# Last block of attention: scores issued two and a half key tiles ahead of the sums of values instead of one and a half

## The chip, the cores and the metric

One NeuronCore of a Trainium2 chip runs the whole program. The metric is the time of one execution on the device in microseconds (us); lower is better. TensorE (PE in the profile) does the matrix products, with its weight loads shown apart (PEld); VectorE is DVE, ScalarE is ACT, GpSimd is POOL, and SyncE (SP) issues most of the DMAs.

## The reference

Two layers in a row, each an attention block followed by an MLP block, with the same weights both times. x is 2048 rows of 640 numbers, there are 32 heads of 20 numbers each, and the MLP is 1536 wide.

```
def _A_ref(x, wqkv, wo):                      # attention
    qkv = (x @ wqkv).reshape(B, S, 3, H, Dh).transpose(2, 0, 3, 1, 4)
    q, k, v = qkv[0], qkv[1], qkv[2]
    scores = einsum("bhqd,bhkd->bhqk", q, k) * (Dh ** -0.5)
    p = softmax(scores, axis=-1)
    o = einsum("bhqk,bhkd->bhqd", p, v)
    return o.transpose(0, 2, 1, 3).reshape(B, S, D) @ wo

def _B_ref(x, w1, b1, w2, b2):                # MLP
    h = relu(x @ w1 + b1)
    return (h * h) @ w2 + b2

for _ in range(2):
    x = x + _A_ref(layernorm(x), A_wqkv, A_wo)
    x = x + _B_ref(layernorm(x), B_w1, B_b1, B_w2, B_b2)
```

## The kernel before, in words

**Stages.** Each layer runs `qkv` (projections), `attention`, then the output projection (`add_heads`) and the MLP (`mlp`). Most operands are kept as a high and a low part, and products are summed from three partial products.

**Blocks of attention.** The work is cut into 32 blocks: 8 groups of four heads times 4 blocks of 512 queries. A block goes over 16 key tiles of 128 keys. For one key tile of a block, TensorE makes the scores of the four heads (each a matrix of 128 keys by 512 queries, one PSUM bank each), ScalarE takes their exponential into a buffer `e` in SBUF, and TensorE then multiplies that with the values and adds to the block's accumulator in PSUM bank 7 (`pv`, line 567: four instructions, one for each head, which the profile counts as eight). A column of ones beside the values gives the sum for the softmax's division. The maxima of the scores, which are subtracted ahead of the exponential, come from a second set of products (line 473) that VectorE reduces; they are made ahead of the block that uses them.

**Order.** The program is written out by hand; each engine runs its instructions in the order written and waits at semaphores. Blocks 0 to 30 follow the strings in `ORDERS`, in which a and b are score products (line 555), m and n are products for the maxima, and V is the sum of values of one key tile. There a score bank is read by one exponential of 512 columns (line 562).

**The last block (31).** When it begins, all maxima are made, so their banks 4 to 6 are free. The block uses `both_heads(p)`: two score products side by side (line 1065) into a pair of banks, and one exponential of 1024 columns over that pair (line 1072). This is called a half here, since it is half of a key tile (two of the four heads); halves are numbered 0 to 31, and half 2k + p belongs to key tile k. Three pairs of banks are used in turn (line 1061), so half n writes the pair that the exponential of half n − 3 has read. Six buffers `e` are used in turn (line 1059), so the exponential of half n writes the buffer that the sum of key tile (n − 6)/2, rounded down, has read.

```
state["bank"] = (state["bank"] + 2) % 6
dst = banks[:, state["bank"] : state["bank"] + 2, :]
```

Halves 0 and 1 are issued among the last instructions of block 30 (line 1098). Line 1102 then issues half 2, and the loop of lines 1103 to 1107 issues the sum of one key tile and then two halves, until the halves run out.

**What hangs on the last block.** `both_heads` calls `begin(i)` when it comes to a new key tile; that writes out the DMAs and the small steps that are due there: the rest of block 30's division (`finish`: a load, a power of −1 on GpSimd, a spread, a gather, a multiplication and a store, at the tiles 4, 6, 7, 9, 11 and 12 after block 30's end), loads of finished heads (`heads`), and at tile 12 four rows of x for the output projection. SyncE takes the DMAs in that order and waits only for what each of them needs. After the block, `add_heads` multiplies the heads with `wo` (line 285 for TensorE, line 1138 for VectorE's addition to x).

Of the kernel before, what the change touches and what calls it, by code (L numbers as in the profile page):

```python
# [39 lines left out]
def tile_layers(  # L40
# [899 lines left out]
    def attention(first, x_src, first_rows):  # L940
# [27 lines left out]
        def begin(i):  # L968

            t, u = divmod(i, NKT)  # L970
            g, qb = divmod(t, NQB)
            if u == 1:
                q_t.pop(t - 1, None)
                if t + 2 < NBLK and t + 2 not in q_t:
                    load_q(t + 2)
            if u % 4 == 1 and qb == 0:
                k_t.pop((g - 1, u // 4), None)
                for h in (0, 1, 2, 3) if g else (0, 1, 2):
                    if g + h < NG and (g + h, u // 4) not in k_t:
                        load_k(g + h, u // 4, True)  # L980
                if g and g + 3 >= NG:
                    del kept[(g - 1) % 4, u // 4]
            if t == 1 and u % 4 == 1:
                load_k(3, u // 4, True)
            if u in (2, 10) and qb == NQB - 1 and g + 1 < NG:
                load_v(g + 1, u // 8)
            if first and t < 16 and u % 6 == 3:
                prep_job()
            if first and t < 16 and u == 8:
                for sp in (w_o, w_1, w_2):  # L990
                    sp.save_full()
                    sp.past(sp.count, sp.got)
            if (t, u) in loads:
                loads[t, u]()
            if t == NBLK - 1 and u == 12:
                first_rows.extend(row_tile(x_src, i) for i in range(4))
            if i in split:
                split.pop(i)()
# [52 lines left out]
        def both_heads(p):  # L1051

            i = state["wide"]
            t, kt = divmod(i, NKT)
            if p == 0 and i > state["begun"]:
                state["begun"] = i
                begin(i)
            es = es_of.setdefault(i, {})
            es[p] = weights[len(e_n) % len(weights)]
            e_n.append(t)  # L1060
            state["bank"] = (state["bank"] + 2) % 6
            dst = banks[:, state["bank"] : state["bank"] + 2, :]
            for par in range(2):
                b = 64 * par
                nc.tensor.matmul(  # L1065
                    dst[:, par, :],
                    k_t[t // NQB, kt // 4][b : b + 62, p, (kt % 4) * P : (kt % 4 + 1) * P],
                    q_t[t][b : b + 62, p, :],
                    start=True,
                    stop=True,  # L1070
                )
            nc.scalar.activation(es[p], dst, AF.Exp, scale=SCALE)  # L1072
            if p:
                state["wide"] += 1
# [24 lines left out]
                else:  # L1099
                    op(o)  # L1100
        assert min(sm_n) == len(todo) and spare == 4
        both_heads(0)
        while state["done"] < last:
            op("V")
            for p in (1, 0):
# [128 lines left out]
    def layer(first, x_a, x_m, x_e, front_0, ahead):  # L1234
        qkv(first, x_a, front_0)
        xs = []
        attention(first, x_a, xs)
        steps = []
        for i in sorted(split):
# [161 lines left out]
```

## Time and profile before

| | |
|---|---|
| median of 3 runs | 3659.83 us (3656.69 to 3662.13) |
| the profiled execution's own time | 3659.64 us |
| its span in the profile | 3657.8 us |
| clock granted to TensorE, mean | 0.998 |
| last block, layer 1 | 1382.40 to 1425.86 us of the span |
| last block, layer 2 | 3197.62 to 3241.06 us of the span |

The two stretches of the last block are counted from the start of the first exponential of 1024 columns to the end of the last sum of values. The profile gives the busy time of each engine, groups of instructions with their mean time, the chain of work that ended last, and rows in order of time. A row of the timeline gives the start, the length, the engine, the line, the operation with output and inputs, the shapes, how many instructions it joins, and in brackets how long the engine was idle just before and what ended that. A merged row ends where its last instruction ends.

### The profile page before, as it was taken

Reading aid. Unit: us, or ns where it says so; the run is one execution under the profiler, and the core shown is the slowest. Engines: PE = TensorE matmul, PEld = TensorE weight load, DVE = VectorE, ACT = ScalarE, POOL = GpSimd, SP = SyncE. Lnnn points to the kernel's source line nnn. Section 1 sums busy time; section 2 is a strip of 40 time slices with the busy share of each in tenths; the row PEclk is TensorE's granted clock in tenths of the full one; section 3 lists DMA queues with packets and bytes.
Section 4 is the critical chain, followed back from the end, with each engine's and each line's share of the span. In section 5 each row is a group of like instructions: output and inputs, shape, how many; then the busy total and the mean of one; then the engine's idle time right before and its main releaser. Section 6 shows DMA issues by size and latency. Waiting matters only on the chain.

```text
span 3657.8 us, 67630 instructions
## 1 busy us (share of the span) xinstructions
PE 3604.9 (99%) x25770; PEld 2153.4 (59%) x25770; DVE 2725.1 (75%) x5039; ACT 2645.2 (72%) x5131; POOL 819.4 (22%) x909
## 2 busy tenths in 40 slices
PE   8999999999999998999999999999999999989999
PEld 7886333343333435999888963334444343369998
DVE  7878999999999992344567789999999999723443
ACT  2778999999999994122227789999999999931221
POOL 6531434211221121111164201211211221101110
PEclk9999999999999999999999999999999999999999
DMA  8866545323211135511277652232232111364111
GB/s 268 279 228 175 170 145 159 102 68 79 56 46 47 50 102 191 208 44 44 80 254 253 205 149 69 70 79 59 64 79 58 44 47 42 110 239 151 44 48 39
DMA packets 254451, 425.03 MB, mean 116 GB/s; under 512 B 60354, under 2 KB 107202, under 8 KB 254126
## 3 DMA queue, kind: packets, MB, share of 16 engines
q1 hardware_dynamic: 253310, 418.35, 36.9%
q8 instruction: 202, 3.31, 0.4%
q10 hardware_dynamic: 816, 2.36, 0.2%
q14 instruction: 123, 1.01, 0.1%
HBM read 260.73 MB, written 159.88 MB: 115 GB/s over the span
## 4 chain that ended last, share of the span: by engine, by line
PE 95%; DVE 2%; ACT 2%; POOL 1%; issue 0%; DMA 0%; SPq 0%; ACTq 0%; DVEq 0%; POOLq 0%
PE banks L567 28%; PE banks L555 19%; PE banks L473 16%; PE banks L285 12%; PE banks L321 10%; PE banks L1201 9%; ACT e L1072 1%; PE banks L1160 0%; DVE mx L485 0%; PE banks L392 0%; PE banks L1065 0%; ACT e L562 0%; DVE bst L243 0%; DVE h L256 0%; DMA q<-d_qk 0%
## 5 line engine op out<-in xcount | busy, mean ns | idle before, releaser
L562 ACT ACTIVATE e<-banks 128x512 f32<-128x512 f32 x3968 | 2049.5, 604 | 65.7 <-PE banks L473 6.8
L485 DVE TENSOR_REDUCE mx<-banks 128x1 f32<-128x512 f32 x3076 | 1931.4, 684 | 212.6 <-PE banks L473 140.7
L473 PE MATMUL banks<-k,q 60*128 60x512 f32 x3587 | 1244.6, 428 | 3.2 <-DVE mx L485 1.4
L567 PE MATMUL banks<-e,vg 128*32 128x512 f32 x8192 | 1091.8, 605 | 29.7 <-ACT e L1072 28.8
L555 PE MATMUL banks<-q,k 62*128 62x512 f32 x3968 | 1118.1, 434 | 1.0 <-DVE mx L502 0.3
L555 PEld LDWEIGHTS banks<-q,k 62*128 62x128 f32 x3968 | 583.8, 185 | 657.3 <-ACT e L562 625.3
L473 PEld LDWEIGHTS banks<-k,q 60*128 60x128 f32 x3587 | 582.0, 184 | 291.6 <-DVE mx L485 217.1
L502 DVE CUSTOM_DVE_ANT_0 rl<-banks,rl 128x512 f32<-128x512 f32 x511 | 333.6, 689 | 102.3 <-PE banks L473 93.5
L567 PEld LDWEIGHTS banks<-e,vg 128*32 128x32 f32 x8192 | 161.2, 108 | 389.9 <-issue 324.8
L321 PE MATMUL banks<-xnT,wqk 64*128 64x512 f32 x2400 | 382.8, 396 | 3.4 <-DVE xnT L256 1.2
L1201 PE MATMUL banks<-w,h 128*128 128x320 f32 x2304 | 349.4, 310 | 0.8 <-DVE h L256 0.7
L494 ACT ACTIVATE rl<-banks 128x512 f32<-128x512 f32 x515 | 273.6, 598 | 101.5 <-PE banks L473 93.3
L1201 PEld LDWEIGHTS banks<-w,h 128*128 128x128 f32 x2304 | 339.3, 188 | 2.5 <-DVE h L256 1.3
L285 PE MATMUL banks<-xnT,w 128*128 128x512 f32 x1440 | 330.0, 389 | 0.0
L1186 ACT ACTIVATE r<-banks,b_t 128x512 f32<-128x512 f32 x96 | 66.2, 689 | 352.8 <-PE banks L285 351.4
L321 PEld LDWEIGHTS banks<-xnT,wqk 64*128 64x128 f32 x2400 | 289.3, 187 | 37.9 <-issue 2.3
L285 PEld LDWEIGHTS banks<-xnT,w 128*128 128x128 f32 x1440 | 269.6, 188 | 55.1
L267 POOL CAST mr<-nt 128x32 fp32r<-128x32 f32 x64 | 13.4, 209 | 1121.5 <-DVE nt L528 1121.3
L611 POOL TENSOR_TENSOR few<-few,minus_t 128x16 f32<-128x16 f32 x62 | 179.8, 2900 | 234.8 <-DMA few<-d_s 234.8
L321 PE MATMUL banks<-wv,xnT 64*128 64x320 f32 x1920 | 199.7, 307 | 0.9 <-ACT mark_t L323 0.9
L321 PEld LDWEIGHTS banks<-wv,xnT 64*128 64x128 f32 x1920 | 187.9, 185 | 2.6 <-ACT mark_t L323 1.6
L1212 DVE TENSOR_TENSOR x<-banks,x 128x320 f32<-128x320 f32 x128 | 62.1, 492 | 168.3 <-PE banks L1201 165.4
(80 smaller groups left out, 2050.9 us busy)
## 6 DMA issues: line engine op xcount, KB each, us to landing
q<-d_qk SPq DMA_DIRECT2D x242, 240.0 KB
d_qk<-ev SPq DMA_DIRECT2D x80, 512.0 KB
k<-d_qk SPq DMA_DIRECT2D x152, 240.0 KB
x<-d_x SPq DMA_DIRECT2D x88, 320.0 KB
d_qk<-ev SPq DMA_DIRECT2D x80, 256.0 KB
d_o<-ot SPq DMA_DIRECT2D x248, 80.0 KB
ot<-d_o SPq DMA_DIRECT2D x38, 512.0 KB
d_v<-v SPq DMA_DIRECT2D x32, 512.0 KB
```

Source lines behind the costliest of these rows:

```text
L285: nc.tensor.matmul(dst, a, b, start=(n == 0), stop=(n == last))
L321: m = nc.tensor.matmul(ch["dst"][:, :width], *pair, start=first, stop=last)
L473: nc.tensor.matmul(dst, q_t[t][b : b + 60, p, sub * P : (sub + 1) * P], k_t[t // NQB, c][b : b + 60, p, :], start=True, stop=True,)
L485: nc.vector.tensor_reduce(maxima(t)[:, 2 * par + p, sub, c : c + 1], dst, axis=AX.X, op=ALU.max)
L494: nc.scalar.activation(res, dst, AF.Relu)
L502: nc.vector.tensor_tensor_reduce(out=r, in0=dst, in1=r, scale=1.0, scalar=LEAST, op0=ALU.add, op1=ALU.max, accum_out=maxima(t)[:, 2 * par ...
L555: nc.tensor.matmul(dst, k_t[t // NQB, kt // 4][b : b + 62, p, (kt % 4) * P : (kt % 4 + 1) * P], q_t[t][b : b + 62, p, :], start=True, stop ...
L562: nc.scalar.activation(es[p][:, par, :], dst, AF.Exp, scale=SCALE)
L567: nc.tensor.matmul(acc[32 * h : 32 * h + 32, :], v_t[t // NQB, kt // 8][:, kt % 8, 32 * h : 32 * h + 32], es[p][:, par, :], start=(kt == 0 ...
L611: nc.gpsimd.tensor_tensor(few, few, minus_t, op=ALU.pow)
L1186: nc.scalar.activation(r, dst, AF.Relu, bias=b1_t[:, f : f + 1])
L1201: nc.tensor.matmul(dst[:, :HALF], hs[f][:, hx, i * P : (i + 1) * P], w_2.piece(at_2(f0 + f, hw, hf)), start=(f == 0 and (hx, hw) == THREE[0]),
```

## The change

One call of `both_heads` ahead of the loop becomes three: half 2, half 3 and half 4 are issued before the sum of key tile 0, where it was half 2 alone. The loop itself is the same, so from there on every sum of key tile k stands behind the halves up to 2k + 4, where it stood behind those up to 2k + 2. The banks, the buffers and the number of instructions are the same. `begin` is called one key tile earlier in relation to the sums; nothing moves in the order of ScalarE, VectorE, GpSimd or SyncE.

```
         assert min(sm_n) == len(todo) and spare == 4
-        both_heads(0)
+        for p in (0, 1, 0):
+            both_heads(p)
         while state["done"] < last:
             op("V")
             for p in (1, 0):
                 if state["wide"] < last:
                     both_heads(p)
```

TensorE at the start of layer 1's last block, before (L567 is the sum of values, four instructions for a key tile; L1065 the scores, two instructions for a half; the first two rows are the last sum of block 30):

```order
L567 MATMUL banks<-e_4750,vg_14074 32x512 x2
L567 MATMUL banks<-e_4749,vg_14074 32x512 x2
L1065 MATMUL banks<-q_14198,k_5125 128x512 x2
L567 MATMUL banks<-e_4752,vg_13921 32x512 [waits DVE_49,Activation_49]
L567 MATMUL banks<-e_4752,vg_13921 32x512
L567 MATMUL banks<-e_4751,vg_13921 32x512 x2
L1065 MATMUL banks<-q_14198,k_5125 128x512 x4
L567 MATMUL banks<-e_4754,vg_13921 32x512 [waits Activation_49]
L567 MATMUL banks<-e_4754,vg_13921 32x512
L567 MATMUL banks<-e_4753,vg_13921 32x512 x2
```

The same place now (L1065 is the same line, since the two lines that were added stand below it):

```order
L567 MATMUL banks<-e_4750,vg_14074 32x512 x2
L567 MATMUL banks<-e_4749,vg_14074 32x512 x2
L1065 MATMUL banks<-q_14198,k_5125 128x512 x2
L1065 MATMUL banks<-q_14198,k_5125 128x512 [waits Activation_49]
L1065 MATMUL banks<-q_14198,k_5125 128x512
L1065 MATMUL banks<-q_14198,k_5125 128x512 [waits Activation_49]
L1065 MATMUL banks<-q_14198,k_5125 128x512
L567 MATMUL banks<-e_4752,vg_13921 32x512 [waits DVE_49]
L567 MATMUL banks<-e_4752,vg_13921 32x512
L567 MATMUL banks<-e_4751,vg_13921 32x512 x2
L1065 MATMUL banks<-q_14198,k_5125 128x512 [waits Activation_49]
L1065 MATMUL banks<-q_14198,k_5125 128x512
```

Halves 3 and 4 now stand ahead of the first sum. Before, the sum of every key tile waited for ScalarE and the scores behind it waited for nothing; now each half of the scores waits for ScalarE (for its pair of banks), and the sums behind them have no wait for ScalarE of their own.

TensorE at the end of the block, before (the row of line 285 is the output projection):

```order
L1065 MATMUL banks<-q_14198,k_5402 128x512 x4
L567 MATMUL banks<-e_4750,vg_14074 32x512 [waits Activation_49]
L567 MATMUL banks<-e_4750,vg_14074 32x512
L567 MATMUL banks<-e_4749,vg_14074 32x512 x2
L1065 MATMUL banks<-q_14198,k_5402 128x512 x2
L567 MATMUL banks<-e_4752,vg_14074 32x512 [waits Activation_49]
L567 MATMUL banks<-e_4752,vg_14074 32x512
L567 MATMUL banks<-e_4751,vg_14074 32x512 x2
L285 MATMUL banks<-wo_14516,ot_14581 128x320 [waits DMAHW4_49]
```

And now:

```order
L567 MATMUL banks<-e_4754,vg_14074 32x512 x2
L567 MATMUL banks<-e_4753,vg_14074 32x512 x2
L1065 MATMUL banks<-q_14198,k_5402 128x512 [waits Activation_49]
L1065 MATMUL banks<-q_14198,k_5402 128x512
L567 MATMUL banks<-e_4750,vg_14074 32x512 [waits Activation_49]
L567 MATMUL banks<-e_4750,vg_14074 32x512
L567 MATMUL banks<-e_4749,vg_14074 32x512 x2
L567 MATMUL banks<-e_4752,vg_14074 32x512 [waits Activation_49]
L567 MATMUL banks<-e_4752,vg_14074 32x512
L567 MATMUL banks<-e_4751,vg_14074 32x512 x2
L285 MATMUL banks<-wo_14516,ot_14581 128x320 [waits DMAHW4_49]
```

The last half of the scores, half 31, stood between the sums of the key tiles 14 and 15; now it stands ahead of both, and these two sums follow one another at the end and wait for ScalarE again.

More of the change, by code (lines that the diff above doesn't have):

```diff
@@ L1101, in attention @@
         assert min(sm_n) == len(todo) and spare == 4
-        both_heads(0)
+        for p in (0, 1, 0):
+            both_heads(p)
         while state["done"] < last:
```

## The prediction, made before the changed kernel was run

> **What bounds the kernel now.** I read the page's busy times and its chain of work first, to see which engine sets the end.
>
> ```profile
> PE 3604.9 (99%) x25770; PEld 2153.4 (59%) x25770; DVE 2725.1 (75%) x5039; ACT 2645.2 (72%) x5131; POOL 819.4 (22%) x909
> PE banks L567 28%; PE banks L555 19%; PE banks L473 16%; PE banks L285 12%; PE banks L321 10%; PE banks L1201 9%; ACT e L1072 1%; PE banks L1160 0%; DVE mx L485 0%; PE banks L392 0%; PE banks L1065 0%; ACT e L562 0%; DVE bst L243 0%; DVE h L256 0%; DMA q<-d_qk 0%
> ```
>
> TensorE is busy for 99% of the span, so nearly nowhere is there time to win. The chain names one exception that belongs to the change: ACT e L1072, the exponentials of the last block. So I asked for the busy time of each engine in the last block of both layers, and, beside them, in a stretch of the full blocks ahead of it.
>
> ```profile
> core 0: us, PE busy (x) PEld busy (x) DVE busy (x) ACT busy (x) POOL busy (x), PEclk, DMA share, GB/s
> 1382.40:1425.86 43.46, 28.59 (x199) 7.43 (x199) 0.69 (x1) 31.13 (x32) 6.06 (x4) 1.00 0.52 173
> 3197.62:3241.06 43.44, 28.56 (x199) 7.42 (x199) 0.69 (x1) 31.13 (x32) 6.07 (x4) 1.00 0.52 173
> 1300.00:1340.00 40.00, 40.00 (x285) 15.90 (x283) 36.32 (x60) 38.99 (x76) 6.97 (x7) 1.00 0.45 144
> ```
>
> The columns are the stretch, its length, and the busy time of each engine. In the last block neither TensorE (28.6 of 43.5 us) nor ScalarE (31.1) is full, while in the full blocks both are. Two engines that both wait are waiting for each other. The rows in order of time show how.
>
> ```profile
> 1381.77 1.06 PE L1065 MATMUL banks<-q,k 62*128 62x512 f32 x4
> 1382.40 2.98 ACT L1072 ACTIVATE e<-banks 128x1024 f32<-128x1024 f32 x3
> 1382.76 1.07 PE L567 MATMUL banks<-e,vg 128*32 128x512 f32 x8
> 1383.76 0.50 PE L1065 MATMUL banks<-q,k 62*128 62x512 f32 x2
> 1384.73 1.07 PE L567 MATMUL banks<-e,vg 128*32 128x512 f32 x8 [0.47 <-DVE o L580]
> ...
> 1387.41 1.06 PE L567 MATMUL banks<-e,vg 128*32 128x512 f32 x8 [0.95 <-ACT e L1072]
> 1388.40 0.73 PE L1065 MATMUL banks<-q,k 62*128 62x512 f32 x4
> 1389.00 1.94 ACT L1072 ACTIVATE e<-banks 128x1024 f32<-128x1024 f32 x2 [0.73 <-PE banks L1065]
> 1390.08 1.06 PE L567 MATMUL banks<-e,vg 128*32 128x512 f32 x8 [0.94 <-ACT e L1072]
> ```
>
> Write S(n) and E(n) for the scores and the exponential of half n, V(k) for the sum of values of key tile k. V(1) starts at 1387.41, S(5) 0.99 later at 1388.40, E(5) 0.60 after that at 1389.00, and V(2), which reads the buffers of E(4) and E(5), at 1390.08, 1.08 later. These make a closed ring of 0.99 + 0.60 + 1.08 = 2.67 us for a key tile: V(2) waits for an exponential whose scores stand behind V(1). The ring comes back each time:
>
> ```profile
> L1072 ACT ACTIVATE e<-banks x64: 1018/1023/1025, 1382.4 to 3238.9; 128x1024 f32<-128x1024 f32 x64
> PE banks L1065: 22.4, 30
> PE banks L567: 28.8, 30
> ```
>
> Of 64 exponentials (1.02 us each) 30 waited for line 1065, and 30 sums waited for line 1072, 28.8 us in all: 15 in each layer.
>
> **The change, part by part.** It adds no instruction and takes none away; it breaks the ring. V(k + 1) now needs E(2k + 3), whose scores stand ahead of V(k). Three things can set the pace then, and I price each for one key tile.
>
> ScalarE: 1.94 us for two in the row at 1389.00, where one takes 1.02, so a start follows the one before by 0.92; a key tile costs 2 × 0.92 = 1.84 us. The second of each two runs while TensorE does a sum (1389.92 to 1390.94 against V(2) from 1390.08), and is not slower for it.
>
> TensorE: a half that has waited lets the sum behind it start 0.42 later (1382.34, the row below, to 1382.76), the sum lets scores start 0.99 later, and the second half of two starts 0.34 after the first (0.73 for both, of which the last matmul takes 0.39). That is 0.42 + 0.99 + 0.34 = 1.75 us. Bounded from above by whole durations with no overlap, it is 1.06 + 2 × 0.50 = 2.06.
>
> ```profile
> 1382.34 0.49 PE L1065 MATMUL banks<-q,k 62*128 62x512 f32 x2
> L1065 PE MATMUL banks<-q,k x128: 385/492/500, 1381.8 to 3238.3; 62*128 62x512 f32 x128
> ```
>
> The banks: with three pairs, S(2k + 6) waits for E(2k + 3), and V(k + 1), which needs the same exponential, stands behind it. So the fifth half issued ahead brings nothing, and holds the sum back by 0.42. Take a steady run with E(2k + 3) at time 0. S(2k + 6) starts at 1.02 + 0.05 = 1.07, V(k + 1) at 1.49, S(2k + 7) at 2.48, and E(2k + 7) could start at 2.48 + 0.60 = 3.08. Its turn on ScalarE is at 4 × 0.92 = 3.68, so 0.6 us are to spare. S(2k + 8) waits for E(2k + 5) until 1.84 + 1.07 = 2.91 and could be read from 3.51; its turn is at 4.60. The next round begins at 2.91 = 1.07 + 1.84, so ScalarE sets the pace, by 1.84 against 1.75.
>
> I take 0.92: the pair at 1389.00 and this last one have it, of 30 in the two layers.
>
> ```profile
> 3236.25 1.94 ACT L1072 ACTIVATE e<-banks 128x1024 f32<-128x1024 f32 x2 [0.73 <-PE banks L1065]
> ```
>
> One row bounds it from above. Exponentials of 512 columns in the full block start 0.523 apart (8.44 for 16, the last 0.60 long), which doubled is 1.05 for a half:
>
> ```profile
> 1297.83 8.44 ACT L562 ACTIVATE e<-banks 128x512 f32<-128x512 f32 x16
> ```
>
> The Trainium skill, "ScalarE: Activation LUTs", section "What ACT_TABLE_LOAD costs", gives 186 ns + 0.833 ns for each column and an overlap of about 93 ns for activations back to back. By that a start would follow after 186 + 853 − 93 = 946 ns, an estimate, and the sum below would lose 2 × 29 × 0.026 = 1.5 us; the trace agrees on one exponential (1.02 against 1.04) and has 0.92 for the distance, which I keep.
>
> Now the ends. E(2) starts where it starts now, since S(2) keeps its place:
>
> ```profile
> 1384.36 1.02 ACT L1072 ACTIVATE e<-banks 128x1024 f32<-128x1024 f32 x1
> 3199.57 1.02 ACT L1072 ACTIVATE e<-banks 128x1024 f32<-128x1024 f32 x1
> ```
>
> (The second is layer 2.) S(3) follows S(2) at 1384.1 into a free pair, and S(4) waits for E(1) until 1384.39, so V(0) slips to 1384.81, by 0.08, which delays no exponential. E(31) starts 29 × 0.92 = 26.68 after E(2), at 1411.04; it ends at 1412.06, and V(15) starts 0.05 later, at 1412.11. V(14) has only E(29) to wait for and is through by then. Now V(15) starts here:
>
> ```profile
> 1424.80 1.06 PE L567 MATMUL banks<-e,vg 128*32 128x512 f32 x8 [1.18 <-ACT e L1072]
> 1425.80 2.47 PE L285 MATMUL banks<-wo,ot 128*128 128x320 f32 x15
> 3240.00 1.06 PE L567 MATMUL banks<-e,vg 128*32 128x512 f32 x8 [1.18 <-ACT e L1072]
> ```
>
> So layer 1 gains 1424.80 − 1412.11 = 12.69 us. In layer 2, V(15) comes at 3199.57 + 26.68 + 1.07 = 3227.32, a gain of 12.68. Together 25.4 us.
>
> **What is late next.** Behind the last sum TensorE begins the output projection without a gap, and stays busy. What the projection reads and does not come from the last block must be there 12.7 us sooner. SyncE's order is unchanged and its DMAs hang on block 30's end, so these keep their times:
>
> ```profile
> 1403.73 2.77 SPq L76 DMA_DIRECT2D d_o<-ot  x4
> 1406.55 1.78 SPq L76 DMA_DIRECT2D x<-in_A_x_dram  x4
> 1408.49 2.81 SPq L76 DMA_DIRECT2D ot<-d_o  x5
> 1411.34 0.74 SPq L76 DMA_DIRECT2D x<-in_A_x_dram  x1
> 1428.30 0.49 DVE L1138 TENSOR_TENSOR x<-banks,x 128x320 f32<-128x320 f32 x1 [1.65 <-PE banks L285]
> 1445.44 4.52 SPq L76 DMA_DIRECT2D w<-d_w  x8
> ```
>
> The rows of x are asked for from 1406.55, behind block 30's store at 1403.73, and VectorE would want the first at 1428.30 − 12.69 = 1415.6, 9 us later. Even if that were late, TensorE could fill eight banks of about 2.2 us each before it stood still. The five loads of heads from 1408.49 are for the last two of the projection's four row blocks. The first eight loads of MLP weights (1445.44) are due after VectorE's additions and move along, to 1432.8; they then start behind the loads above, not among them. I cost this at nothing; if the cover is gone, what is lost is what TensorE then waits in `add_heads`, at most the 25.4.
>
> **Rivals.** *A smaller gain, TensorE or a slower exponential sets the pace.* At 2.06 us a key tile, V(15) ends at 1384.73 + 15 × 2.06 + 1.06 = 1416.7, where it is 1425.86 now: 9.2 a layer, 18.3 in all, 3641.3. At 1.05 for an exponential the loss is 2 × 29 × 0.13 = 7.5, which gives 3641.8. For it speaks that TensorE has only 0.09 us to spare in a key tile by my count; against it, that its overlaps are measured. The Trainium skill, "TensorE: Matmul & The Clock Gate", part 2, says that matmuls stay in program order, so a half that waits for its banks does hold the sum behind it; the sum with it is the one above, 1.75.
>
> *Given back behind the block.* If the rows of x came only at about 1441, all would be lost: 3659.6, the same. The same comes out if the change did not do what it says, because the scores wait for their banks; but E(2k + 3), for which S(2k + 6) waits, would then have to be late itself, and it has 0.6 us to spare.
>
> *Slower.* Banks are slices of one tile. If a half waited for the newest exponential before it and not for its own pair's, S(n), E(n) and S(n + 1) would follow one another: 0.60 + 1.02 + 0.05 = 1.67 for a half, where it is 2.67 / 2 = 1.335 now, which is the point that decides. Over the 28 halves from 4 to 31 that is 28 × 0.335 = 9.4 us a layer, 18.8 in all: 3678.4. Against it: S(2) ran at 1383.76 while exponentials ran without a break from 1382.40 to 1385.38.
>
> **How the numbers follow.** The profiled execution took 3659.64 us, 1.84 beyond its span, which I leave as it is; it lies 0.19 below the median of 3659.83. 3659.64 − 25.36 = 3634.3, against the median 3634.5; I say 3634.4. Chances: the forecast 0.78, the smaller gain 0.14, no change 0.04, slower 0.04. The range takes in the smaller gain (to 3641.8) and, at both ends, the spread of the three runs, 3.1 below the median and 2.3 above: 3630 to 3644. About 0.2%, 7.3 us, is what a measurement of this kernel can tell from no change; the first two cases lie beyond it, so faster 0.92, same 0.04, slower 0.04.
>
> **What would show it.** Right: the exponentials of line 1072 run without a gap from the third on, 0.92 apart; hardly a wait for line 1065 is left in place of 30; the scores wait for line 1072, and the sums no longer, but for the last two; the last block takes 30.8 us where it took 43.5. Wrong: gaps between exponentials with scores as their releaser, or a wait of line 285 or of line 1138 for a DMA right behind the block.

## The result, and the profile after

| | before | changed |
|---|---|---|
| median, first runs | 3660.98 us (3656.69 to 3662.60, 4 runs) | 3632.51 us (3630.76 to 3635.09, 4 runs) |
| ratio, 95% interval | | 0.9925 (0.9907 to 0.9942) |
| the profiled execution's own time | 3659.64 us | 3635.09 us |
| its span | 3657.8 us | 3633.3 us |
| last block, layer 1 and layer 2 | 43.46 and 43.44 us | 30.67 and 30.67 us |

The forecast was 3634.4 us and a last block of 30.8 us. Two lines of the profile of the changed kernel, its busy times and its chain of work (line 1202 is the old line 1201):

```profile
PE 3610.4 (99%) x25770; PEld 2155.8 (59%) x25770; DVE 2724.9 (75%) x5039; ACT 2641.1 (73%) x5131; POOL 820.6 (23%) x909
PE banks L567 28%; PE banks L555 19%; PE banks L473 16%; PE banks L285 12%; PE banks L321 10%; PE banks L1202 9%; DMA q<-d_qk 1%; PE banks L1065 1%; PE banks L1161 0%; PE banks L392 0%; ACT e L562 0%; ACT e L1072 0%; DVE bst L243 0%; DVE h L256 0%; SPq L76 0%
```

ACT e L1072 has gone from the places that count. The two stretches of the last block in the changed kernel, in the columns of before (stretch, length, busy PE, PEld, DVE, ACT, POOL, clock, DMA share, GB/s):

```profile
1382.60:1413.27 30.67, 29.89 (x199) 8.36 (x199) 0.69 (x1) 29.55 (x32) 6.06 (x4) 1.00 0.51 160
3185.79:3216.46 30.67, 29.89 (x199) 8.38 (x199) 0.69 (x1) 29.55 (x32) 6.08 (x4) 1.00 0.51 158
```

ScalarE is now busy for 29.55 of 30.67 us. The rows in order of time:

```profile
1382.60 13.97 ACT L1072 ACTIVATE e<-banks 128x1024 f32<-128x1024 f32 x15
...
1386.97 1.06 PE L567 MATMUL banks<-e,vg 128*32 128x512 f32 x8
...
1387.97 0.91 PE L1065 MATMUL banks<-q,k 62*128 62x512 f32 x4
1388.37 0.18 PEld L1065 LDWEIGHTS banks<-q,k 62*128 62x128 f32 x2 [0.22 <-ACT e L1072]
...
1388.81 1.07 PE L567 MATMUL banks<-e,vg 128*32 128x512 f32 x8
...
1390.64 1.07 PE L567 MATMUL banks<-e,vg 128*32 128x512 f32 x8
```

Fifteen of the 32 exponentials stand in one row without a gap where there were pairs with 0.73 us between them. The sums start at 1386.97, 1388.81 and 1390.64, 1.83 us apart where it was 2.67. The second half behind each sum waits for ScalarE (the weight load at 1388.37), and the sum itself does not. The view of line 1072 counts who waits:

```profile
L1072 ACT ACTIVATE e<-banks x64: 1019/1186/1392, 1382.6 to 3214.0; 128x1024 f32<-128x1024 f32 x64
PEld banks L1065: 30.2, 56
PEld banks L567: 3.8, 4
PE banks L567: 1.5, 2
```

The 30 waits of the exponentials for line 1065 are gone. In their place 56 halves of the scores wait for their banks, and only the last sums of each layer wait for an exponential.

### The profile page after: what moved, and what is told of

It is laid out like the page before. It is cut to its first block, busy times and chain, and to the rows that moved or that the text cites. A ratio compares the mean times of both kernels' runs of the same rounds, so it can differ in the third digit from the quotient of the medians.

```text
span 3633.3 us, 67626 instructions
## 1 busy us (share of the span) xinstructions
PE 3610.4 (99%) x25770; PEld 2155.8 (59%) x25770; DVE 2724.9 (75%) x5039; ACT 2641.1 (73%) x5131; POOL 820.6 (23%) x909
## 3 DMA queue, kind: packets, MB, share of 16 engines
q1 hardware_dynamic: 253310, 418.35, 37.1%
## 4 chain that ended last, share of the span: by engine, by line
PE 95%; DVE 1%; ACT 1%; DMA 1%; POOL 1%; issue 1%; SPq 0%; ACTq 0%; DVEq 0%; POOLq 0%
PE banks L567 28%; PE banks L555 19%; PE banks L473 16%; PE banks L285 12%; PE banks L321 10%; PE banks L1202 9%; DMA q<-d_qk 1%; PE banks L1065 1%; PE banks L1161 0%; PE banks L392 0%; ACT e L562 0%; ACT e L1072 0%; DVE bst L243 0%; DVE h L256 0%; SPq L76 0%
## 5 line engine op out<-in xcount | busy, mean ns | idle before, releaser
L567 PE MATMUL banks<-e,vg 128*32 128x512 f32 x8192 | 1093.0, 606 | 1.5 <-ACT e L1072 1.5
L567 PEld LDWEIGHTS banks<-e,vg 128*32 128x32 f32 x8192 | 161.6, 108 | 357.7 <-issue 330.7
```

The lines of the kernel that those rows point to most:

```text
L567: nc.tensor.matmul(acc[32 * h : 32 * h + 32, :], v_t[t // NQB, kt // 8][:, kt % 8, 32 * h : 32 * h + 32], es[p][:, par, :], start=(kt == 0 ...
```

## The experiments

All are read by the length of the last block, from the first of its exponentials to the end of its last sum; it came out within 0.3 us in the two layers of one execution, while whole executions of one kernel lie up to 7 us apart (before: 3655.58 to 3662.78 in 9 runs).

**How far ahead.** In two kernels the scores run four and six halves ahead of the sums, where before had three and the change has five.

```
-        for p in (0, 1, 0):
+        for p in (0, 1):             # the other kernel: (0, 1, 0, 1)
             both_heads(p)
         while state["done"] < last:
             op("V")
-            for p in (1, 0):
+            for p in (0, 1):
```

> The scores are issued two key tiles (four halves) ahead of the sums, between the one and a half of before and the two and a half of the change. Theory (three pairs of banks and ScalarE at 0.92 us an exponential set the pace; the fifth half only waits for its banks): the last block takes 30.9 us in each layer, as with five halves (30.67), and the exponentials run without a gap; by the count in steps of 0.99 + 0.05 + 0.60 an exponential has only about 0.1 us to spare, so a small gap now and then would not speak against it. Rival (each half issued ahead brings its share of the gain): halfway between 43.46 and 30.67, about 37 us.

> The scores are issued three key tiles (six halves) ahead. Theory: ScalarE is full, so 30.7 us for the last block again; the sums only start later, behind a half that waits for the exponential after the one that the sum needs. Rival (a half that waits for its banks holds the sums up and is paid for): another 0.9 us or so for each key tile, about 13 us more, 44 us.

The last block of each, four ahead and then six ahead:

```profile
1379.99:1410.79 30.80, 28.32 (x199) 7.34 (x199) 0.69 (x1) 29.65 (x32) 6.08 (x4) 1.00 0.55 173
```

```profile
1379.54:1410.22 30.68, 29.75 (x199) 8.46 (x199) 0.69 (x1) 29.54 (x32) 6.07 (x4) 1.00 0.53 165
```

Four ahead takes 30.80 us, six ahead 30.68, five 30.67; three took 43.46. The gain comes in one step between three and four, so both rivals fall: it doesn't grow with the lead beyond that step, and the halves that wait for banks cost nothing. With four ahead it is the sums again that wait, and no gap is counted in front of the exponentials:

```profile
L1072 ACT ACTIVATE e<-banks x64: 1018/1096/1104, 1380.0 to 3209.5; 128x1024 f32<-128x1024 f32 x64
PEld banks L567: 19.6, 32
PE banks L567: 1.9, 4
```

So a wait of TensorE is no cost in itself; what counts is whether ScalarE has an exponential to go on with. The 0.13 us between four and five is one exponential that comes late: with four ahead, the fifth of each layer ends 1.05 us after the fourth (1383.87 and 1384.92 in layer 1), and all later ones follow by 0.92. The two whole times, one run each beside 3659.43 for before, were 3630.38 and 3629.97 us.

**The ring, by a shorter exponential.** In before and in the changed kernel, the exponentials are made over half of their columns.

```
-            nc.scalar.activation(es[p], dst, AF.Exp, scale=SCALE)
+            nc.scalar.activation(es[p][:, 0, :], dst[:, 0, :], AF.Exp, scale=SCALE)
```

> The kernel before, with the exponentials of the last block on the first 512 of their 1024 columns (those of two of the four heads are left out; the sums read what stands in the buffers). Theory (a ring of sum 0.99, scores 0.60, exponential 1.02 + 0.05 in each key tile): an exponential of 512 columns takes 0.60, the ring gets 0.42 shorter for each key tile, and the block takes 37.1 us where it took 43.46. Rival (TensorE's own work sets the pace): no change.

> The changed kernel, with the exponentials of the last block on the first 512 of their 1024 columns (those of two of the four heads are left out). Theory (ScalarE sets the pace by 1.84 us a key tile, TensorE is next with 1.67 to 1.75): the exponentials get 0.42 shorter each, but the block only goes from 30.67 to about 27.4 us, where TensorE is busy without a gap. Rival 1 (TensorE sets the pace already): 30.7. Rival 2 (ScalarE alone sets it, TensorE has much room): about 18.5.

The last block of layer 1 in the kernel before with the shorter exponential, by engine:

```profile
1381.68:1418.54 36.86, 36.47 (x199) 9.41 (x199) 0.69 (x1) 17.50 (x32) 6.09 (x4) 1.00 0.60 204
```

ScalarE's rows in it:

```profile
1394.49 1.09 ACT L1072 ACTIVATE e<-banks 128x512 f32<-128x512 f32 x2 [1.14 <-PE banks L1065]
1396.73 1.09 ACT L1072 ACTIVATE e<-banks 128x512 f32<-128x512 f32 x2 [1.15 <-PE banks L1065]
```

Rows in order of time of the same kernel, which show the sum (weight loads and products) and the scores beside them:

```profile
1394.56 1.64 PE L567 MATMUL banks<-e,vg 128*32 128x512 f32 x8
1395.14 0.15 PEld L567 LDWEIGHTS banks<-e,vg 128*32 128x32 f32 x6 [0.44 <-ACT e L1072]
1396.13 0.74 PE L1065 MATMUL banks<-q,k 62*128 62x512 f32 x4
```

The same two views of the changed kernel with the shorter exponential:

```profile
1381.71:1408.88 27.17, 27.17 (x199) 7.65 (x199) 0.69 (x1) 17.37 (x32) 6.07 (x4) 1.00 0.49 146
```

```profile
1393.81 1.08 ACT L1072 ACTIVATE e<-banks 128x512 f32<-128x512 f32 x2 [0.57 <-PE banks L1065]
1395.47 1.08 ACT L1072 ACTIVATE e<-banks 128x512 f32<-128x512 f32 x2 [0.57 <-PE banks L1065]
```

Before, two exponentials started every 2.67 us and ScalarE stood still for 0.73 of them. With the shorter ones they start every 2.24 us (1394.49 to 1396.73), although ScalarE is idle for over 1.1 us: each 0.42 us taken from one exponential came off the ring whole, once for each key tile. The block fell from 43.46 to 36.86 (37.1 expected). That is a ring, and no full engine. TensorE looks full there, with 36.47 of 36.86 us, but the same products fit into 27.17 us in the next kernel: here the first head of each sum reads a buffer that no exponential writes here: it starts ahead (1394.56), the other three heads wait for the exponential (1395.14), and the row lasts 1.64 us where a whole sum takes 1.06. From those three heads on, the ring has its old terms, 0.99 to the scores at 1396.13 and 0.60 to the exponential at 1396.73.

In the changed kernel the same cut takes only 30.67 to 27.17 us (27.4 expected). The pairs now start 1.66 us apart, and TensorE is busy for all of the 27.17 us: it is TensorE's own pace, 1.66 us a key tile, which stands 0.17 to 0.18 below ScalarE's. Both rivals (30.7 and 18.5) fall. The whole times of these two kernels, one run each, were 3645.34 and 3626.30 us beside 3659.43 for before.

**The banks.** Two pairs of banks in turn instead of three:

```
-            state["bank"] = (state["bank"] + 2) % 6
+            state["bank"] = (state["bank"] + 2) % 4
```

> The changed kernel with two pairs of banks in turn in place of three. Theory: a half then waits for the exponential of two halves before; the second half behind each sum comes 0.3 us too late for its turn on ScalarE, a key tile takes 2.00 us where it takes 1.84, and the last block 33.0 us where it takes 30.67. Rival (the lead alone matters, not the banks): 30.7. Rival (a half waits for the newest exponential before it, whatever its banks): the same as with three pairs, 30.7.

The last block of this kernel by engine, and behind it ScalarE's rows:

```profile
1382.72:1415.76 33.04, 30.62 (x199) 8.33 (x197) 0.69 (x1) 30.37 (x32) 6.08 (x4) 1.00 0.58 183
```

```profile
1391.66 3.79 ACT L1072 ACTIVATE e<-banks 128x1024 f32<-128x1024 f32 x4 [0.23 <-PE banks L1065]
1395.68 3.79 ACT L1072 ACTIVATE e<-banks 128x1024 f32<-128x1024 f32 x4 [0.22 <-PE banks L1065]
```

It takes 33.04 us (33.0 expected; 33.28 in layer 2). Four exponentials start every 4.02 us, and behind every fourth there is a gap of 0.22: 2.01 us a key tile. So each half does wait for its own pair of banks, and not for the newest exponential, and the third pair is worth 2.4 to 2.6 us a layer here. The time agrees better than the count: a half comes too late only behind every second sum, and four exponentials lose 0.34 us in all (4.02 against 4 × 0.92), where the expectation had a late half behind each sum. The whole time was 3639.89 us in one run, beside 3658.86 for before.

**The last sum.** At the end TensorE stands still until the last exponential is done. This kernel puts the two heads that need the exponential before it first:

```
-                pv(state["acc"], t, u, es_of.pop(i))
+                pv(state["acc"], t, u, es_of.pop(i), (1, 0, 3, 2) if i == last - 1 else (3, 2, 1, 0))
```

> The changed kernel with the very last sum of values of a layer in another order of heads: 1 and 0, which need the exponential of half 30, ahead of 3 and 2, which need half 31. Theory (at the end TensorE stands still for 0.76 us until half 31 is done, and a sum of two heads is half of the 1.0 us): the last block takes 30.2 us where it takes 30.67, about 1 us in both layers together. Rival (the eight instructions of a sum run side by side and cannot be split): no change.

The last block of this kernel by engine, and behind it rows in order of time at its end (weight loads, which start with the matmuls that they serve):

```profile
1382.13:1412.79 30.66, 30.63 (x199) 8.49 (x199) 0.69 (x1) 29.55 (x32) 6.08 (x4) 1.00 0.51 154
```

```profile
1410.82 0.14 PEld L567 LDWEIGHTS banks<-e,vg 128*32 128x32 f32 x4 [0.73 <-ACT e L1072]
1411.74 0.14 PEld L567 LDWEIGHTS banks<-e,vg 128*32 128x32 f32 x4 [0.77 <-ACT e L1072]
...
1412.72 0.45 PEld L285 LDWEIGHTS banks<-wo,ot 128*128 128x128 f32 x3 [0.84 <-issue]
```

My theory falls: 30.66 us, nothing won. The first two heads did run early, from 1410.82, but the other two, from 1411.74, take 0.98 us until the projection can start at 1412.72, as long as the four heads of a whole sum (0.99). So here a sum of half the heads is not half a sum, as the rival said: its eight instructions are recorded with about 0.6 us each (592 to 618 ns), and the whole sum takes 1.06, so they run side by side. The whole time was 3632.12 us in one run, beside 3658.86 for before.

**Work in the gaps.** Can TensorE's spare time be used? This kernel issues the first chain of the output projection inside the last block, into the free bank 6, and leaves it out behind it.

```
+        po = banks[:, 6, :]
+        early = [
+            (ready[0][k][:, hx, :P], w_o.piece(k * 4 + hw * 2))
+            for k in range(KD)
+            for hx, hw in THREE
+        ]
...
+            for _ in range({last - 1: 5, last: 0}.get(state["done"], 1 if len(early) > 5 else 0)):
+                pair = early.pop(0)
+                nc.tensor.matmul(
+                    po[:, :HALF], *pair, start=len(early) == 3 * KD - 1, stop=not early
+                )
```

> The changed kernel, and the first of the 32 chains of the output projection (15 matmuls of 128x320, 2.2 us) is issued inside the last block, into bank 6, which nothing uses there: one matmul behind the scores of each of the first ten key tiles, and five ahead of the very last sum, where TensorE stands still for 0.76 us. Theory (TensorE needs 1.67 us of the 1.84 us that ScalarE takes for a key tile, so that one matmul of about 0.15 us fits): the last block stays at 30.7 to 31.0 us, the projection behind it gets 2.2 us shorter, and the kernel gains about 2 us a layer, 4 in all, against the changed kernel. Rival (TensorE has only the 0.09 us to spare that the count with 0.42 behind a waiting half gives): the ten matmuls cost 0.06 us each and a little more, the block takes 31.3 us or more, and half of it is gone.

The changed kernel was run again on the same chip:

> The changed kernel once more, on the same chip as the one above and beside as many runs of the kernel before. Theory (all that the change does is done in the last block, 12.8 us in each layer): 25.6 us faster than before, ratio 0.9930. Rival (the 28.5 us between the medians of the first runs hold some 3 us that are won elsewhere): ratio 0.9922.

The last block with the early projection by engine, and behind it TensorE's rows (line 1117 is the matmul that was moved in, line 593 the first product behind the block):

```profile
1382.27:1414.39 32.12, 32.10 (x213) 10.08 (x213) 0.69 (x1) 30.39 (x32) 6.07 (x4) 1.00 0.56 171
```

```profile
1388.65 0.41 PE L1117 MATMUL banks<-wo,ot 128*128 128x320 f32 x1
1388.99 1.07 PE L567 MATMUL banks<-e,vg 128*32 128x512 f32 x8
1389.99 0.73 PE L1065 MATMUL banks<-q,k 62*128 62x512 f32 x4
1390.65 0.42 PE L1117 MATMUL banks<-wo,ot 128*128 128x320 f32 x1
1391.00 1.07 PE L567 MATMUL banks<-e,vg 128*32 128x512 f32 x8
...
1415.63 1.13 PE L593 MATMUL banks<-o,sums_t 128*128 128x512 f32 x2 [1.24 <-DVE x L1152]
```

The block got 1.4 us longer (30.72 and 30.68 us in the changed kernel's second profile), as the rival said and more. TensorE has no gap, and a key tile takes 2.01 us (1388.99 to 1391.00): 1.00 for the sum, 0.66 for two halves, and 0.35 for the one matmul between scores and sum, where I had counted 0.15 from the projection's own stretch (2.2 us for 15). So the spare 0.17 us of a key tile does not hold one matmul, and TensorE sets the pace. Nor did the projection get 2.2 us shorter: without its first chain TensorE stands still behind the block and waits for VectorE, 1.24 us in layer 1 (the last row) and 0.84 in layer 2. The projection's second chain starts 33.92 us after the start of layer 1's block, against 33.40 in the changed kernel's second profile, and 33.52 against 33.37 in layer 2, so nothing was won. As a whole the kernel had a ratio of 0.9929 (0.9915 to 0.9943), 3632.95 us, beside 0.9931 (0.9918 to 0.9943), 3634.43 us, for the changed kernel again; that is no difference that can be measured.

The changed kernel's second measurement (5 runs beside 9 of before, 3659.45 us) is 25.0 us faster than before. That speaks for the theory, 0.9930 with 25.6 us from the two blocks alone; but the rival's 0.9922 lies in the interval as well.

## Why the prediction was right

**The ring and its end.** The forecast was that a key tile would cost ScalarE's 1.84 us in place of the ring's 2.67. It cost 1.83, and the experiments with the shorter exponential show the ring before and its absence after. The block came out at 30.67 where the sum said 30.8, and the gain at 12.8 us a layer where it said 12.7. That 3634.4 lies within 0.1 us of the second median (3634.43) is luck, with executions of one kernel up to 7 us apart.

**The three prices.** ScalarE's 0.92 us held; ends of exponentials followed one another by 0.917 (below). The figures of the Trainium skill ("ScalarE: Activation LUTs", section "What ACT_TABLE_LOAD costs") gave an estimate of 0.946; the measurement is 3% below it. TensorE's 1.75 a key tile was counted with a waiting half in it, and no run has TensorE at that pace; without any wait it is 1.66, and the bound of 2.06 lies far above it. The banks: the 0.6 us to spare were there.

```profile
1408.13 0.91 PE L1065 MATMUL banks<-q,k 62*128 62x512 f32 x4
```

This half of the scores, half 29, could be read 0.60 us later, from 1408.73. The last exponential ended at 1412.15, so that of half 29 ended two steps of 0.917 earlier, at 1410.32, and its 1.02 us began at 1409.30. With two pairs of banks the same kind of count gave 33.0 against 33.04 measured.

**The fifth half.** I said that it brings nothing and only holds the sum up. Four halves ahead without it take 0.13 us longer, the one late exponential at the start of the block; that is all that it brings. The prediction had put this at nothing.

**What is late next.** Nothing, in `add_heads`: the first addition came at 1415.70, released by TensorE, no DMA held TensorE up in the projection, and SyncE asked for the rows of x at the old time, and for the MLP's weights 12.6 us earlier.

```profile
1406.53 1.80 SPq L76 DMA_DIRECT2D x<-in_A_x_dram  x4
1415.70 0.49 DVE L1139 TENSOR_TENSOR x<-banks,x 128x320 f32<-128x320 f32 x1 [1.64 <-PE banks L285]
1432.89 4.08 SPq L76 DMA_DIRECT2D w<-d_w  x8
```

**The time.** Of the 28.5 us between the first medians, 25.6 are the two blocks. The other 3 are no more than the spread of executions: the interval of the first measurement holds 25.6, and the second measurement had 25.0. In the profiled executions, 24.5 us lie between the spans; the largest part of what is missing to 25.6 lies between the two blocks. From the end of the first to the start of the second it took 1771.76 us before, 1772.52 in the changed kernel's first profile and 1770.95 in its second. There, at the start of the second layer's attention, the clock granted to TensorE was lower for longer in the first profile of the changed kernel (0.50 from 2131 to 2136) than in that of before (0.57 from 2144 to 2147). The same stretch of the span in the changed kernel's first and second profile:

```profile
2131.00:2136.00 5.00, 5.00 (x25) 1.49 (x23) 2.97 (x6) 3.19 (x7) 0.46 (x2) 0.50 0.52 152
```

```profile
2131.00:2136.00 5.00, 5.00 (x37) 2.00 (x40) 4.28 (x9) 4.89 (x11) 0.46 (x2) 1.00 0.33 99
```

The same program was given half the clock in one and the whole in the other, and did 25 matmuls against 37, so this is not the change. What decides it was not tried.

## What to carry to other kernels

Two engines that are both idle for part of a loop may be in a ring, each waiting for the other; add up the ring from rows in order of time, cut it by issuing the producer's work far enough ahead, and price what comes next, which here was the fullest engine. One step was enough here: from three halves to four, and a fifth brought only 0.13 us and a sixth nothing, since ScalarE was already full. Count the spare time of the other engine in the sequence in which the work will stand: a matmul of 0.15 us in its own chain cost 0.35 between two others. And look at what the moved work covered where it stood: here its absence left a wait of about 1 us.

## What the runs showed of the hardware that was not expected

**Rows of a full ScalarE grow.** The second and the last exponential of layer 1's block in the changed kernel:

```profile
1383.52 1.02 ACT L1072 ACTIVATE e<-banks 128x1024 f32<-128x1024 f32 x1
...
1410.76 1.39 ACT L1072 ACTIVATE e<-banks 128x1024 f32<-128x1024 f32 x1
```

The recorded length goes from 1.02 to 1.39 us over 30 exponentials, though nothing gets slower: the second ends at 1384.54 and the last at 1412.15, 27.61 us for 30 steps, which is 0.920 each with the wait of 0.1 in front of the third, and 0.917 without it. From the fourth on, the recorded starts run ahead at 0.903 apart. Lengths of rows on a full ScalarE are not prices; distances of ends are. With two pairs of banks, where ScalarE has a gap behind every fourth, they stay between 1.02 and 1.06; with four halves ahead, where ScalarE is just as full, they grow to 1.10 and no further. Why the starts run ahead was not tried.

**Half a sum takes as long as a whole one:** two of the four heads took 0.98 us, all four 0.99, each head with weights of 128x32.
